# Second level of the down product for chunk 0 of experts 1 to 3, with the down-weight sums right after the up-weight sums

## The chip, the cores and the metric

The kernel runs on one core of a Trainium2 chip. The metric is the device time of one execution in microseconds (us); lower is better. The engines of the core appear in the profile as PE (TensorE matmul), PEld (TensorE weight load), DVE (VectorE), ACT (ScalarE), POOL (GpSimd) and SP (SyncE, which here only issues DMAs).

## The reference

Two blocks follow each other. The first is an attention without softmax with a normalised output; the second weighs four expert networks by probabilities. All arrays are float32.

```python
kv  = einsum('bhsd,bhse->bhde', k, v)              # 8 batches, 8 heads, 576 rows, 64 columns
o   = einsum('bhsd,bhde->bhse', q, kv)
x   = (o / sqrt(mean(o*o, -1) + 1e-6) * g_norm)    # then reshaped to x: 4608 x 512
p   = domain_probs / (domain_probs.sum(-1) + 1e-9) # 4608 x 4
out = sum over e of p[:, e] * (relu(x @ w1[e]) @ w2[e])   # w1: 4 x 512 x 1024, w2: 4 x 1024 x 512
```

Nearly all arithmetic is in the two products per expert, called the up product (x @ w1) and the down product (h @ w2).

## The kernel before

**Tiling and stages.** The 4608 rows of x are cut into NCH = 9 chunks of 512 rows. A stage `s = e*9 + c` is the work of expert `e` (0 to 3) on chunk `c` (0 to 8), so there are 36 stages. Expert 0 also computes the attention that makes the chunks and keeps them, with their sums, in DRAM; experts 1 to 3 load them again (`x_again`).

**Strassen's scheme.** Products are made by the Strassen-Winograd scheme: seven products in place of eight, at the price of sums of the operands before and of the products after. In `up` (from line 851) two levels are used in every stage but the first: 7 outer times 7 inner products, each of two 128x128x128 matmuls (line 881). The down product exists in two forms:

- `down` (from line 1077) uses one level: for each of two halves of rows `t`, seven products (`MERGED` order) of four matmuls with 256 columns each (line 1095). `merge` (lines 1042 and 1049) takes each product from its PSUM bank, scales it by the probability and adds it to the output tile.
- `down_deep` (from line 1117) uses two levels. Seven outer products in four groups, (1, 6), (7, 5), (4, 2) and (3), each with seven inner products of two matmuls with 128 columns per outer product (line 1170). Before them VectorE or GpSimd makes sums of the hidden tiles (`ht`, by `combine`, line 360); between and after them ScalarE copies (line 1198) and VectorE adds (lines 1206 and 1236) put the products together.

**Which stage uses which.** Expert 0 always uses `down`; experts 1 to 3 use `down` for chunks 0 and 8 and `down_deep` for chunks 1 to 7.

**Weights.** While stage `s` with `c = 8` of expert `e` runs, the weights of expert `e + 1` are loaded and summed. `weights_1` loads the four quarters of w1 and makes 4 first-level and 28 second-level sums (buffers `w1y`). `weights_2` loads the four quarters of w2 and makes 4 first-level sums; the function `inner` that it returns makes the 28 second-level sums of w2 (128x256 each, buffers `w2y`), which only `down_deep` reads. The `w2y` buffers are made of room that the attention leaves free: `kv`, `kvbd` and `x_rem`.

**What sets the order.** The program is recorded as operations with a key (a place in units of stages) and an estimate of their cost, and `Plan.layout` turns them into one order per engine. Matmuls go by key, taking the next one that is ready within 0.7 of a stage; VectorE, ScalarE and GpSimd take the ready operation that is due first; SP issues loads by key, and only when a buffer is free. Sums marked `port` (lines 360 and 1236) are kept from running at the same time on VectorE and GpSimd. Buffers (`big`, 29 and later 33 of 128x1024; PSUM kinds `u1`, `u2`, `db`, `ab` of two banks each) are given out in that order too. The down product of stage `s` has keys from `s + 1.2` on: it is interleaved with the up product of stage `s + 1`.

**Bank order.** In `down_deep` ScalarE copies one product into a second PSUM bank and PE accumulates onto the copy (the seed). The seed must land in a bank that PE has already written wide enough; `inner_last` holds a reference to earlier groups for that.

Of the kernel before, what the change touches and what calls it, by code (L numbers as in the profile page):

```python
# [230 lines left out]
def kernel(  # L231
# [36 lines left out]
    nc = tc.nc  # L268
# [3 lines left out]
    P = nc.NUM_PARTITIONS  # L272
# [4 lines left out]
    NCH = B + 1  # L277
    HN = NT // 2
# [13 lines left out]
    ident = const.tile([P, P], F32, name="ident")  # L292
# [41 lines left out]
    plan = Plan()  # L334

    def pe(products, columns, passes=2):
        return {"PE": passes * products * (0.008 + 0.0008125 * columns) + 0.003}
# [4 lines left out]
    def act(n):  # L342
        return {"ACT": 0.155 + 0.00088 * n}

    def either(n):
        return {"DVE": 0.155 + 0.00104 * n, "POOL": 0.15 + 0.00225 * n}
# [9 lines left out]
    def combine(key, cost, out_, a, b, op, reads, writes):  # L356

        plan.add(
            key, cost,
            lambda eng: adder(eng).tensor_tensor(out=out_(), in0=a(), in1=b(), op=op),  # L360
            reads=reads, writes=writes, port=True,
        )

    def load(key, buf, dst, src, kb, reads=(), also=()):
        plan.add(
            key, SPC, lambda eng: nc.sync.dma_start(out=dst(), in_=src), reads=reads,
            parts=[buf] + list(also), kb=kb,
        )
# [37 lines left out]
    def two(ap):  # L406
        return ap.rearrange("p (k t) -> p k t", k=2)
# [5 lines left out]
    def w2_src(e, uh, dh):  # L413
        rows = moe_w2[e][uh * HF:(uh + 1) * HF, dh * HN:(dh + 1) * HN]
        return rows.rearrange("(kt p) d -> p kt d", p=P)
# [50 lines left out]
    def weights_2(e, key, step, deep):  # L466

        f = {n: Buf("big", f"w2_{e}_{n}") for n in (1, 12, 2, 3, 5, 6, 7, 4)}
        for i, (n, uh, dh) in enumerate(((1, 0, 0), (2, 1, 0), (12, 0, 1), (3, 1, 1))):
            load(  # L470
                key + i * step, f[n],
                lambda n=n: f[n].ap[:].rearrange("p (k d) -> p k d", k=4),
                w2_src(e, uh, dh), 512,
            )

        def form(k_, o, a, b, op):
            combine(
                k_, either(1024), lambda: f[o].ap[:], lambda: f[a].ap[:], lambda: f[b].ap[:], op,
                [f[a], f[b]], [f[o]],
            )  # L480

        form(key + 4 * step, 5, 12, 1, ALU.subtract)
        form(key + 5 * step, 6, 3, 5, ALU.subtract)
        form(key + 6 * step, 7, 3, 12, ALU.subtract)
        form(key + 7 * step, 4, 2, 6, ALU.subtract)
        w2f[e] = f

        def inner():
            w2q[e] = {}
            for j, m in enumerate(OUTER):  # L490
                x, y = f[m], Buf("w2y", f"w2y_{e}_{m}")
                parts = {}
                for n, (dq, uq) in ((1, (0, 0)), (2, (0, 1)), (21, (1, 0)), (4, (1, 1))):
                    parts[n] = (x, lambda x=x, dq=dq, uq=uq: x.ap[:].rearrange(
                        "p (k d) -> p k d", k=4)[:, 2 * uq:2 * uq + 2, dq * P:(dq + 1) * P])
                for n, at in ((5, 0), (6, 1), (3, 2), (7, 3)):
                    parts[n] = (y, lambda y=y, at=at: two(y.ap[:, at * HN:(at + 1) * HN]))
                for o, a, b, op in (
                    (5, 21, 4, ALU.add), (7, 1, 21, ALU.subtract), (6, 5, 1, ALU.subtract),
                    (3, 2, 6, ALU.subtract),  # L500
                ):
                    combine(
                        deep + j / 7, either(HN), parts[o][1], parts[a][1], parts[b][1], op,
                        [parts[a][0], parts[b][0]], [y],
                    )
                w2q[e][m] = parts

        return inner
# [330 lines left out]

    hidden = {}  # L840
    summed = {}
    last, inner_last = [], []

    def four(b):

# [271 lines left out]
    def down_deep(s, e, c):  # L1117
# [8 lines left out]
        for i, group in enumerate(((1, 6), (7, 5), (4, 2), (3,))):  # L1126
# [34 lines left out]
            for j, mm in enumerate(ORDER):  # L1161
                key = at + n * j / 49
                ps = bank[{2: 2, 5: 5, 3: 5}.get(mm, 1)]

                def product(eng, group=group, mm=mm, ps=ps, forms=forms):
                    for o, m in enumerate(group):
                        b, at = forms[m][mm]
                        for kt in range(2):
                            col = at * HN + kt * P
                            nc.tensor.matmul(  # L1170
                                ps.ap[:, o * P:(o + 1) * P], lhsT=b.ap[:, col:col + P],
                                rhs=w2q[e][m][mm][1]()[:, kt, :],
                                start=(mm in (1, 5) and o == 0 and kt == 0), stop=(kt == 1),
                                skip_group_check=True,
                            )

                op = plan.add(
                    key, pe(2 * n, P), product,
                    reads=[b for m in group for b in (w2q[e][m][mm][0], forms[m][mm][0])]
                    + ([ps] if mm == 2 else []),  # L1180
                    **{"parts" if mm == 2 else "writes": [ps]},
                    after=inner_last[-2:-1] if mm == 1 else seeds if mm == 5 else (),
                )
                op.marks, op.seed = (ps, n * P), mm == 2
                if mm == 3:
                    inner_last.append(op)

                def cell(tq, dq, pair=pair, n=n):
                    return pair.ap[:].rearrange(
                        "p (o b i t) -> p o b i t", o=2, b=2, i=2)[:, 0:n, tq, dq, :]  # L1190

                def group_of(ap, n=n):
                    return ap[:, 0:n * P].rearrange("p (o t) -> p o t", o=n)

                def copy(where, key=key, ps=ps, n=n, group_of=group_of, **kw):
                    return plan.add(
                        key - 0.4, act(n * P),
                        lambda eng: nc.scalar.activation(  # L1198
                            out=where(), in_=group_of(ps.ap), func=ACT.Copy),
                        reads=[ps], **kw,  # L1200
                    )

                def total(tq, dq, src, add_, key=key, n=n, cell=cell, group_of=group_of, outs=outs):
                    plan.add(
                        key - 0.4, dve(n * P),
                        lambda eng: nc.vector.tensor_tensor(
                            out=cell(tq, dq), in0=group_of(src.ap), in1=group_of(add_.ap),
                            op=ALU.add,
                        ),
                        reads=[src, add_], parts=outs,  # L1210
                    )

                if mm == 1:
                    seeds = [copy(lambda b=bank[2], g=group_of: g(b.ap), parts=[bank[2]])]
                elif mm in (6, 7):
                    snap[mm] = Buf("snap", f"ds{mm}_{s}_{i}")
                    copy(lambda b=snap[mm], g=group_of: g(b.ap), parts=[snap[mm]])
                if mm == 2:
                    copy(lambda cell=cell: cell(0, 0), parts=outs)
                elif mm == 7:  # L1220
                    total(1, 1, bank[5], snap[7])
                elif mm == 4:
                    copy(lambda cell=cell: cell(0, 1), parts=outs)
                elif mm == 3:
                    total(1, 0, ps, snap[6])
# [60 lines left out]
    inner = {}  # L1286
    for e in range(E):
        for c in range(NCH):
            s = e * NCH + c
            if e == 0 and c + 1 < B:  # L1290
                attention(c + 1, s - 0.1, 0.8, s + 0.5)
            if e + 1 < E and c == NCH - 1:
                weights_1(e + 1, s + 0.0, 0.12, s + 0.3)()
                inner[e + 1] = weights_2(e + 1, s + 1.0, 0.12, s + 2.5)
            if s + 1 < E * NCH:
                if e == 0 and c + 1 < NCH:
                    x_views[s + 1] = x_forms(c + 1, s + 0.7)
                else:
                    x_views[s + 1] = x_again((c + 1) % NCH, s + (0.05 if e else 0.6), 0.13)
            if s:  # L1300
                up(s, e, x_views.pop(s))
            if c == 1 and e:
                inner[e]()
            if e and 1 <= c < NCH - 1:
                down_deep(s, e, c)
            else:
                down(s, e, c)
# [54 lines left out]
```

## Time and profile before

| What | Value |
|---|---|
| Median of 9 runs | 1737.31 us (1736.73 to 1737.81) |
| The profiled execution's own time | 1737.34 us |
| Its span, first to last instruction | 1735.6 us |
| Granted TensorE clock, mean | 0.998 |
| PE busy | 1725.9 us (99% of the span) |
| PEld busy | 1649.1 us (95%) |
| DVE busy | 1163.3 us (67%) |
| ACT busy | 922.7 us (53%) |
| POOL busy | 640.2 us (37%) |
| DMA | 220.89 MB, mean 127 GB/s |

The busy time of an engine is the time in which at least one of its instructions runs. Matmuls overlap in the array, so a group's mean length (275 ns for 128 columns) is longer than the distance between two starts; the cost of a matmul on a busy PE is read from the chain of work or from whole stages. A float32 matmul appears as two records. Some matmul records can be missing, so counts of matmuls are taken from the program and not from the trace.

### The profile page before, as it was taken

The page shows a single profiled execution, that of the slowest core. Times are in us where ns is not written, and L with a number is a line of the kernel's source. Part 1 is how long each engine was busy: PE and PEld are TensorE (multiplying, and loading weights), DVE is VectorE, ACT ScalarE, POOL GpSimd, SP SyncE. Part 2 cuts the span into 40 slices and gives each one's busy share as a digit, 9 for nine tenths or more (in the row PEclk, how much of TensorE's full clock was granted, in tenths as well). Part 3 has the DMA queues.
Part 4 walks back from the last instruction along what each step waited for, and adds up shares of the span by engine and source line. Part 5 has one row for each costly group of instructions (what it writes and reads, how often), then busy time and mean ns, then how long its engine had stood idle before and what let it go on. Part 6 is the DMA issues. An engine that isn't in the chain of part 4 may idle for free.

```text
span 1735.6 us, 37757 instructions
## 1 busy us (share of the span) xinstructions
PE 1725.9 (99%) x15074; PEld 1649.1 (95%) x15074; DVE 1163.3 (67%) x1836; ACT 922.7 (53%) x2240; POOL 640.2 (37%) x603
## 2 busy tenths in 40 slices
PE   9999999999999999999999999999999999999998
PEld 7699999999999999999999999999999999999997
DVE  4755655565673567777786567777786567777774
ACT  3354544554444455656555456566655456565652
POOL 2421322133334523333345523333346623333331
PEclk9999999999999999999999999999999999999999
DMA  9756443633333343434455434444456434444442
GB/s 237 220 159 192 156 125 122 192 139 135 135 134 98 107 101 101 117 102 118 126 169 130 104 98 110 110 110 110 119 158 150 110 98 110 111 110 107 113 99 49
DMA packets 148592, 220.89 MB, mean 127 GB/s; under 512 B 49600, under 2 KB 90816, under 8 KB 148416
## 3 DMA queue, kind: packets, MB, share of 16 engines
q1 hardware_dynamic: 133312, 191.21, 34.8%
q0 software_dynamic: 15104, 27.27, 10.9%
q8 instruction: 118, 1.93, 0.5%
q14 instruction: 58, 0.48, 0.1%
HBM read 145.30 MB, written 73.14 MB: 126 GB/s over the span
## 4 chain that ended last, share of the span: by engine, by line
PE 99%; POOL 0%; ACT 0%; DVE 0%; issue 0%; POOLq 0%
PE u L881 44%; PE db L1095 17%; PE db L1170 16%; PE ab L1170 10%; PE ab L1095 4%; PE u L968 2%; PE ab L634 1%; PE ab L678 1%; PE ab L1311 1%; PE ab L620 1%; PE ab L660 1%; PE db L660 0%; POOL rt L551 0%; PE ab L722 0%; PE ab L704 0%; PE ab L738 0%
## 5 line engine op out<-in xcount | busy, mean ns | idle before, releaser
L360 DVE TENSOR_TENSOR big<-big,big 128x1024 f32<-128x1024 f32 (+1 forms) x457 | 481.4, 1068 | 42.0 <-ACT big L864 28.0
L881 PE MATMUL u<-xf,big 128*128 128x128 f32 x3392 | 491.9, 275 | 0.0
L881 PEld LDWEIGHTS u<-xf,big 128*128 128x128 f32 x3392 | 439.0, 192 | 3.7
L881 PE MATMUL u<-xf,w1y 128*128 128x128 f32 x2652 | 387.9, 275 | 0.0
L908 DVE TENSOR_TENSOR big<-u,snap 128x256 f32<-128x256 f32 x460 | 194.1, 422 | 285.4 <-PE u L881 195.0
L881 PEld LDWEIGHTS u<-xf,w1y 128*128 128x128 f32 x2652 | 344.4, 192 | 3.3
L900 ACT ACTIVATE snap<-u 128x256 f32<-128x256 f32 x490 | 188.1, 384 | 257.0 <-PE u L881 222.1
L1095 PE MATMUL db<-big,big 128*128 128x256 f32 x1176 | 278.4, 380 | 2.1 <-DVE big L560 2.1
L900 ACT ACTIVATE big<-u 128x256 f32<-128x256 f32 x460 | 176.5, 384 | 122.6 <-PE u L881 85.1
L1095 PEld LDWEIGHTS db<-big,big 128*128 128x128 f32 x1176 | 212.9, 191 | 26.0 <-DVE big L560 2.3
L360 POOL TENSOR_TENSOR big<-big,big 128x256 f32<-128x256 f32 (+1 forms) x140 | 184.3, 1331 | 128.0 <-DVE big L360 43.5
L864 ACT ACTIVATE big<-big 128x1024 f32<-128x1024 f32 x135 | 141.9, 1051 | 6.5 <-DVE big L360 3.8
L1236 POOL TENSOR_TENSOR big<-big 128x512 f32<-128x512 f32 x21 | 26.6, 1268 | 257.5 <-DVE big L360 188.6
L360 POOL TENSOR_TENSOR big<-big 128x512 f32<-128x512 f32 (+1 forms) x57 | 67.0, 1177 | 134.0 <-DVE big L360 100.2
L1065 POOL DMA_DIRECT2D out_dram<-big x106 | 95.0, 967 | 52.0 <-ACT big L1042 32.9
L1170 PE MATMUL db<-big,big 128*128 128x128 f32 x760 | 108.3, 275 | 0.4 <-ACT snap L1198 0.4
L1198 ACT ACTIVATE snap<-db 128x256 f32<-128x256 f32 (+1 forms) x168 | 60.0, 357 | 86.4 <-PE db L1170 81.6
L900 ACT ACTIVATE u<-u 128x256 f32<-128x256 f32 x245 | 90.8, 371 | 25.4 <-PE u L881 4.5
L1170 PEld LDWEIGHTS db<-big,big 128*128 128x128 f32 x760 | 96.3, 192 | 0.6 <-ACT snap L1198 0.6
L547 POOL TENSOR_SCALAR ss<-ss 128x16 f32<-128x16 f32 (+2 forms) x26 | 6.4, 247 | 241.4 <-DVE ss L540 241.1
L1049 DVE SCALAR_TENSOR_TENSOR big<-db,p_all,big 128x256 f32<-128x256 f32 x74 | 35.7, 483 | 87.3 <-PE db L1095 85.6
L1170 PE MATMUL ab<-kv,big 128*128 128x128 f32 x624 | 89.1, 275 | 0.0
(202 smaller groups left out, 2654.5 us busy)
## 6 DMA issues: line engine op xcount, KB each, us to landing
xf<-x SPq DMA_DIRECT2D x108, 512.0 KB, 3.5
out_dram<-big POOLq DMA_DIRECT2D x90, 256.0 KB, 5.6
xf<-x_h SPq DMA_DIRECT2D x81, 256.0 KB, 3.0
xf<-x SPq DMA_DIRECT2D x81, 256.0 KB, 3.1
x<-xf SPq DMA_DIRECT2D x36, 512.0 KB, 6.7
big<-in_moe_w_dram SPq DMA_DIRECT2D x27, 512.0 KB, 5.2
small<-in_q_dram SPq DMA_DIRECT2D x72, 128.0 KB, 4.6
kv<-in_k_dram SPq DMA_DIRECT2D x30, 288.0 KB, 5.0
```

Of the source, the lines that this page charges most:

```text
L360: lambda eng: adder(eng).tensor_tensor(out=out_(), in0=a(), in1=b(), op=op),
L864: lambda eng: nc.scalar.activation(out=b.ap[:], in_=b.ap[:], func=ACT.Relu),
L881: nc.tensor.matmul(ps.ap[:, u * P:(u + 1) * P], lhsT=w1f[e][m][mm][1]()[:, u * P:(u + 1) * P], rhs=views[m][mm][1](), start=(mm in (1, 5) ...
L900: lambda eng: nc.scalar.activation(out=where(), in_=ps.ap[:, 0:HN], func=ACT.Copy),
L908: lambda eng: nc.vector.tensor_tensor(out=block(whole, a, t), in0=src.ap[:, 0:HN], in1=add_.ap[:], op=ALU.add),
L968: nc.tensor.matmul(bank.ap[:], lhsT=two(w.ap[:])[:, kt, ut * P:(ut + 1) * P], rhs=two(xh[dh].ap[:])[:, kt, :], start=(dh == kt == 0), stop ...
L1049: lambda eng: nc.vector.scalar_tensor_tensor(out=cell(i, half), in0=ap(), scalar=prob(), in1=cell(i, half), op0=ALU.mult, op1=ALU.add,),
L1065: nc.gpsimd.dma_start(out=dst, in_=cell(i)[parts, :], accum_op=ALU.add)
L1095: nc.tensor.matmul(ps.ap[:, 0:HN], lhsT=four(h[m])[:, kt // 2, t, kt % 2, :], rhs=w2f[e][m].ap[:, kt * HN:(kt + 1) * HN], start=(m in (1, ...
L1170: nc.tensor.matmul(ps.ap[:, o * P:(o + 1) * P], lhsT=b.ap[:, col:col + P], rhs=w2q[e][m][mm][1]()[:, kt, :], start=(mm in (1, 5) and o == ...
L1198: lambda eng: nc.scalar.activation(out=where(), in_=group_of(ps.ap), func=ACT.Copy),
L1236: lambda eng: adder(eng).tensor_tensor(out=whole(to), in0=whole(a), in1=whole(b), op=ALU.add),
```

## The change

Chunk 0 of experts 1, 2 and 3 uses `down_deep` as well. For that the 28 second-level sums of w2 are recorded one chunk earlier and with earlier keys, the four loads of w2 move from `s + 1.0 ...` to `s + 0.6 ...` (`s` is the last chunk's stage of the expert before) and are 0.1 instead of 0.12 of a stage apart, and the 28 sums move from `s + 2.5` on to `s + 1.3` on. Since in expert 1 the first `down_deep` no longer follows a `down` that has filled the `ab` banks, a new operation `prime` of four 128x128 matmuls with the identity fills them once.

```diff
-    last, inner_last = [], []
+    last, inner_last, primed = [], [], []
...
-                    after=inner_last[-2:-1] if mm == 1 else seeds if mm == 5 else (),
+                    after=(inner_last[-2:-1] or primed) if mm == 1 else seeds if mm == 5 else (),
...
-                inner[e + 1] = weights_2(e + 1, s + 1.0, 0.12, s + 2.5)
+                inner[e + 1] = weights_2(e + 1, s + 0.6, 0.1, s + 1.3)
...
-            if c == 1 and e:
+            if c == 0 and e:
                 inner[e]()
-            if e and 1 <= c < NCH - 1:
+            if e and c < NCH - 1:
+                if not primed:
+                    banks = [Buf("ab", f"prime{i}") for i in range(2)]
+
+                    def prime(eng, banks=banks):
+                        for b in banks:
+                            nc.tensor.matmul(b.ap[:, 0:P], lhsT=ident[:], rhs=ident[:], start=True,
+                                             stop=False, skip_group_check=True)
+                            nc.tensor.matmul(b.ap[:, P:HN], lhsT=ident[:], rhs=ident[:], start=False,
+                                             stop=True, skip_group_check=True)
+
+                    primed.append(plan.add(s + 1.1, pe(4, P), prime, writes=banks))
+                    primed[0].marks = banks[0], HN
                 down_deep(s, e, c)
             else:
                 down(s, e, c)
```

## The prediction

> **What bounds the kernel now.** I read the chain of work that ended last first. On the page it says by engine, then by line:
>
> ```profile
> PE 99%; POOL 0%; ACT 0%; DVE 0%; issue 0%; POOLq 0%
> ```
>
> TensorE is the chain. Whether it also waits inside that chain is answered by the waits of TensorE (who waited for whom, us in total, times, longest):
>
> ```profile
> PE db L1095 <- DVE big L560: 2.1, 1, 2.1
> PE ab L1311 <- POOL ident masks.py:199: 1.4, 1, 1.4
> PE u L881 <- ACT snap L900: 0.6, 1, 0.6
> PE u L881 <- ACT u L900: 0.5, 1, 0.5
> ```
>
> Asked again by windows, all of this lies in the first 90 us; from 460 us to the end, experts 1 to 3, one wait of 0.4 us is left. There the time is the sum of its matmuls, so the price of a matmul is the distance between starts. The chain between 905 and 997 us (start, us, what) has the prices:
>
> ```profile
> 917.11 1.73 PE db L1095 x8
> ...
> 931.11 1.78 PE u L881 x16
> ```
>
> Eight records of 128x256 take 1.73 us: 0.216 each. Sixteen of 128x128 take 1.78: 0.111 each. A float32 matmul is two records.
>
> Whole stages are the better measure, since they hold every gap. The ScalarE copies of line 900 are 35 per up product, so the 1st, 36th, ... of them mark the stages. Busy time by windows (us, then busy PE, PEld, DVE, ACT, POOL with counts, clock, DMA share, GB/s) of two stages with two-level down products, and of the two stages in which the down products of expert 1's last chunk and expert 2's first chunk run:
>
> ```profile
> 729.60:817.20 87.60, 87.60 (x787) 87.60 (x787) 66.39 (x101) 53.40 (x135) 31.32 (x29) 1.00 0.43 109
> 905.10:997.40 92.30, 92.30 (x635) 86.94 (x634) 54.94 (x76) 45.15 (x106) 52.30 (x59) 1.00 0.49 121
> ```
>
> Both are full of TensorE at the same clock, both hold two up products, and they differ by 4.70 us: **a first-level down product costs 2.35 us more than a second-level one.**
>
> **The sum, part by part.**
>
> *Matmuls replaced.* A first-level product is 14 products of 4 matmuls, 112 records x 0.216 = 24.2 us. A second-level one is 49 x 2 matmuls, 196 records x 0.1117 = 21.9 us (0.1117 is 87.60 / 784, as such a pair of stages holds 4 x 196 records). By records the gain is 2.3, by stages 2.35. Three stages change: 3 x 2.35 = **7.05 us removed**. The order of the built changed kernel has just these counts: 168 matmuls of line 1095 fewer and 294 of line 1170 more.
>
> A rule of the Trainium skill speaks against this edit. "Perfetto Trace Analysis", section Matmuls, holds that larger matmuls are more efficient than smaller ones. The rows agree in sign: 0.1117 / 128 = 0.87 ns per column against 0.216 / 256 = 0.84, some 3%. Were the small ones as cheap per column, the gain would be 3 x 3.0 = 9 us; with the rows it is the 7 us above. The saving of an eighth of the arithmetic outweighs it.
>
> *The new priming matmuls.* Four, so 8 records of 128 columns: 8 x 0.1117 = **0.9 us added**, once. They wait for both `ab` banks; in the order they stand where expert 0's last down product uses `db` alone, so I take no wait. Bounds: 0.4 (if one record each) to 2.5 (if they also wait for one 0.4 us copy at each bank).
>
> *Vector work of the new form.* Per changed stage VectorE or GpSimd get 7 sums of 512 columns (0.68 us, row of line 360) and 14 of 256 (0.41), 7 of line 1236 (0.69) and 8 of line 1206 (six of 0.42, two of 0.28), and lose 6 merges of line 1049 (0.48): 10.5 + 4.8 + 3.1 - 2.9 = 15.5 us of VectorE time. ScalarE gains 20 copies of about 0.36. Nothing of it is on the chain while it keeps ahead. The stage in which it will lie, up of chunk 1 beside down of chunk 0, is the third line here; an ordinary two-level stage is the fourth:
>
> ```profile
> 861.80:905.10 43.30, 43.30 (x390) 43.30 (x390) 37.00 (x55) 25.38 (x66) 21.29 (x22) 1.00 0.58 171
> 905.10:951.30 46.20, 46.20 (x327) 43.73 (x326) 30.88 (x42) 24.02 (x58) 26.58 (x26) 1.00 0.58 138
> 951.30:997.40 46.10, 46.10 (x310) 43.21 (x310) 24.06 (x34) 21.14 (x49) 25.72 (x34) 1.00 0.40 103
> 1040.60:1085.30 44.70, 44.70 (x403) 44.70 (x402) 33.57 (x51) 27.99 (x70) 16.28 (x15) 1.00 0.43 107
> ```
>
> VectorE is busy 24.1 of 46.1 us and most of GpSimd's 25.7 are second-level sums of w2, which move away. What is left is like the fourth line, in which TensorE does not wait. So I put this at nothing.
>
> *The w2 sums, moved one stage forward.* They go into the second line: the first five of the 28 begin there already (GpSimd rows from 933.9 us on), so 23 come in addition, 23 x 0.41 = 9.4 us if VectorE makes them, 23 x 0.73 = 16.8 if GpSimd does. The built order gives VectorE 18 and GpSimd 10 of the 28 for experts 2 and 3. 18 x 0.41 = 7.4 brings VectorE to 38.3 of 46.2 us, a share of 83%; GpSimd stays below its 26.6, as it loses some up-weight sums too. The first line has 37.0 of 43.3, 85%, and no wait of TensorE. The two together matter as well, for they hold each other up: in the first line 128x1024 sums on VectorE last 1.37 us in the mean, and one of them 2.31, against 1.21 for the shortest.
>
> "SBUF — State Buffer", section "two separate sides", calls the port pair that VectorE and GpSimd share an exclusive lock. By that the two busy times of the second line would be added: 30.9 + 26.6 + 9.4 = 66.9 us against 46.2, and TensorE would wait 20 us per expert; but already before they add up to 57.5 without a wait, since sums from PSUM and scaled merges run beside.
>
> In the order all up-weight sums (`w1y`) on VectorE now stand ahead of all down-weight sums for experts 2 and 3, and are done a seventh of a stage earlier than before (14 on VectorE, 7 on GpSimd, against 11 and 10). What waits behind the moved sums is only the next down product, which needs them. Cost nothing, with a bound of 16.8 us per expert.
>
> *Where TensorE could catch up.* One place of the order is new: three to four sevenths into the up product of chunk 0 of experts 2 and 3, TensorE has 20 up matmuls in a row, and then five first-level down products with only two up matmuls between. Before, 6 to 8 up matmuls and one product of four alternate. From the beginning of the stage before up to the end of this place TensorE has 69.8 us of matmuls in both orders (by the two prices), VectorE's queue holds 55.6 us against 51.9 (shortest lengths). In the seventh itself it is 9.6 against TensorE's 11.8. So VectorE still is ahead, by less: I allow **0.2 us** in all for it, between 0 and 5 us per expert, nearest to the second line's zero.
>
> *The w2 loads.* Four issues per expert, 512 KB each; in experts 2 and 3 each stands four issues earlier in SP's queue, ahead of loads of x. The DMA share was 0.58 in the first line; 2 MB more in 43 us is 49 GB/s on 171. SP spends its time waiting for TensorE to free a buffer of x (1022 us in all), so it is ahead of need. Nothing; a load of w2 that waits for its buffer would hold back x by some such wait, 11.1 us at the longest.
>
> Sum, against the profiled execution: 1737.34 - 7.05 + 0.9 + 0.2 = 1731.4. Its own time is within 0.03 of the median.
>
> **The rivals.** About 0.2%, 3.5 us, is what a measurement of this kernel tells from no change: faster is below 1733.8, slower above 1740.8.
>
> *Part is given back (1732.5 to 1737).* VectorE is late at the new place of experts 2 and 3, and TensorE waits 1 to 3 us in each. For it: the 85% line, and the bunched order. Against it: zero waits before.
>
> *The first groups wait for the w2 sums: no gain.* The last of these sums stand in VectorE's queue 0.2 of a stage after the first second-level matmuls are due. If each of the three new products waited as long as it saves, 2.35 us, only the priming would be left: 1738.2. This is also the case in which the change does not do what it says. Against it: the order has up matmuls between them, which TensorE takes while they are ready.
>
> *Slower.* The moved sums and VectorE's own totals (line 908, which frees the up banks) collide at the new place: if GpSimd makes the sums at 0.73 and VectorE is held for most of it, 16.8 us per expert stand ahead of totals, and the five down products cover 5 x 1.73 = 8.6 of it. Two such transitions lose 2 x 8.2 = 16.4: 1731.2 + 16.4 = 1747.6. It decides from 4.8 us per transition on. Against it: the order leaves GpSimd only 10 of the 28.
>
> **How the numbers follow.** The forecast, with under 1.2 us lost, 60%: 1730.3 (priming at 0.4, 2.45 per stage) to 1732.5. Part given back 22%, about two fifths of it still below 1733.8. No gain 10%, slower 8%. Faster is 0.60 + 0.09 + 0.01 for a small piece of the third case = 0.70; same 0.22; slower 0.08. The range must leave out no more than 2 in 10: from 1730.3 through most of the second case to 1736.5.
>
> **What would show it.** Right: TensorE's waits still under 6 us; the two stages around each expert's beginning last 90 us instead of 92.3, the new one 43.8; 33 to 34 us of VectorE in it. Wrong: new lines "PE u L881 <- DVE big" or "PE ab/db L1170 <- DVE kv" with some us, and a VectorE near full in the stage before. A gain well beyond 7 us would mean that the price per stage was misread.

## The result and the profile after

| What | Before | After |
|---|---|---|
| Median of the runs made side by side | 1737.19 us (30 runs) | 1731.42 us (10 runs, 1730.84 to 1731.73) |
| Ratio after to before | | 0.9966, 95% interval 0.9958 to 0.9974 |
| Profiled execution, own time | 1737.34 us | 1730.86 us |
| Its span | 1735.6 us | 1729.1 us |
| DVE busy | 1163.3 us (67%) | 1223.0 us (71%) |
| POOL busy | 640.2 us (37%) | 617.4 us (36%) |

The kernel became 5.77 us faster; 1731.4 had been forecast. On the page of the changed kernel the chain of work that ended last is still TensorE:

```profile
PE 99%; POOL 1%; DVE 0%; ACT 0%; issue 0%; POOLq 0%
```

The waits of TensorE in the changed kernel, from 400 us to the end (who waited for whom, us in total, times, longest), have only the line that the kernel before has too:

```profile
PE db L1170 <- ACT snap L1198: 0.4, 1, 0.4
```

So no wait for the added work shows on the chain. Where the time went is seen in the stages, marked as before by every 35th copy of line 900. Busy time by windows of the changed kernel (columns as in the prediction): the last chunk of expert 1, then the two stages that hold the down products of that chunk and of expert 2's first chunk, one by one and together:

```profile
859.90:903.20 43.30, 43.30 (x390) 43.30 (x389) 37.02 (x57) 23.74 (x64) 21.52 (x20) 1.00 0.66 195
903.20:949.40 46.20, 46.20 (x326) 43.72 (x326) 38.21 (x59) 26.06 (x61) 24.01 (x24) 1.00 0.51 115
949.40:993.50 44.10, 44.10 (x382) 43.69 (x381) 35.78 (x56) 23.39 (x58) 16.08 (x18) 1.00 0.33 97
...
903.20:993.50 90.30, 90.30 (x706) 87.41 (x706) 73.99 (x115) 49.45 (x118) 40.09 (x42) 1.00 0.42 106
```

The pair lasts 90.30 instead of 92.30 us. The stage after it became shorter as well; before and after:

```profile
997.40:1040.60 43.20, 43.20 (x374) 42.79 (x373) 30.08 (x46) 23.09 (x57) 12.74 (x12) 1.00 0.36 99
993.50:1036.40 42.90, 42.90 (x386) 42.90 (x385) 32.80 (x51) 25.43 (x66) 15.01 (x14) 1.00 0.44 111
```

By the unrounded marks that is 1.96 and 0.33 us, **2.29 us per expert**. The same two differences stand in the traces at the beginnings of experts 1 and 3; the first stage of expert 1, which has the priming, is 0.89 us longer, and the other stages from 460 us up to the mark of the last one last alike to 0.01 us. The columns of VectorE and GpSimd show the price that stays hidden: VectorE went from 30.88 to 38.21 us in the second line and from 24.06 to 35.78 in the third, GpSimd from 25.72 to 16.08 in the third.

The new place of the order is where the chain in order of time of the changed kernel (start, us, what) has these pieces:

```profile
915.63 4.47 PE u L881 x40
920.10 1.73 PE db L1095 x8
921.83 0.44 PE u L881 x4
922.27 1.73 PE ab L1095 x8
924.00 5.18 PE db L1095 x24
929.18 0.89 PE u L881 x8
```

They are the 20 up matmuls (40 records), then five one-level products with two up matmuls between. Each piece starts where the one ahead ends: 5.18 us is 24 x 0.216. The bunch cost nothing.

### The profile page after: what moved, and what is told of

Its sections match the earlier page's. It is cut to its first block, busy times and chain, and to the rows that moved or that the text cites. A ratio compares the mean times of both kernels' runs of the same rounds, so it can differ in the third digit from the quotient of the medians.

```text
span 1729.1 us, 38448 instructions
## 1 busy us (share of the span) xinstructions
PE 1719.2 (99%) x15334; PEld 1651.5 (96%) x15334; DVE 1223.0 (71%) x1968; ACT 939.5 (54%) x2300; POOL 617.4 (36%) x561
## 4 chain that ended last, share of the span: by engine, by line
PE 99%; POOL 1%; DVE 0%; ACT 0%; issue 0%; POOLq 0%
PE u L881 45%; PE db L1170 19%; PE db L1095 15%; PE ab L1170 12%; PE ab L1095 2%; PE u L968 2%; PE ab L634 1%; PE ab L1323 1%; PE ab L620 1%; PE ab L678 1%; PE ab L660 1%; POOL rt L551 0%; PE db L660 0%; PE ab L722 0%; PE ab L704 0%; PE ab L738 0%
## 5 line engine op out<-in xcount | busy, mean ns | idle before, releaser
L360 DVE TENSOR_TENSOR big<-big,big 128x1024 f32<-128x1024 f32 (+1 forms) x449 | 440.8, 995 | 35.0 <-ACT big L864 23.8
L881 PE MATMUL u<-xf,big 128*128 128x128 f32 x3104 | 453.0, 275 | 0.0
L881 PEld LDWEIGHTS u<-xf,big 128*128 128x128 f32 x3104 | 401.3, 192 | 2.2
L908 DVE TENSOR_TENSOR big<-u,snap 128x256 f32<-128x256 f32 x430 | 181.3, 422 | 235.6 <-PE u L881 176.2
L1095 PEld LDWEIGHTS db<-big,big 128*128 128x128 f32 x1136 | 205.9, 190 | 25.4 <-DVE big L560 2.3
L1170 PE MATMUL db<-big,big 128*128 128x128 f32 x1056 | 146.8, 275 | 0.4 <-ACT snap L1198 0.4
L1170 PEld LDWEIGHTS db<-big,big 128*128 128x128 f32 x1056 | 132.1, 192 | 0.6 <-ACT snap L1198 0.6
L1198 ACT ACTIVATE snap<-db 128x256 f32<-128x256 f32 x192 | 68.5, 357 | 99.9 <-PE db L1170 95.0
L1170 PE MATMUL db<-kv,big 128*128 128x128 f32 x804 | 114.6, 275 | 0.0
L1170 PEld LDWEIGHTS db<-kv,big 128*128 128x128 f32 x804 | 102.1, 192 | 0.1
L1206 DVE TENSOR_TENSOR big<-ab,snap 128x256 f32<-128x256 f32 x140 | 59.1, 422 | 57.4 <-ACT snap L1198 31.9
```

Source lines behind the costliest of these rows:

```text
L881: nc.tensor.matmul(ps.ap[:, u * P:(u + 1) * P], lhsT=w1f[e][m][mm][1]()[:, u * P:(u + 1) * P], rhs=views[m][mm][1](), start=(mm in (1, 5) ...
L908: lambda eng: nc.vector.tensor_tensor(out=block(whole, a, t), in0=src.ap[:, 0:HN], in1=add_.ap[:], op=ALU.add),
L1095: nc.tensor.matmul(ps.ap[:, 0:HN], lhsT=four(h[m])[:, kt // 2, t, kt % 2, :], rhs=w2f[e][m].ap[:, kt * HN:(kt + 1) * HN], start=(m in (1, ...
L1170: nc.tensor.matmul(ps.ap[:, o * P:(o + 1) * P], lhsT=b.ap[:, col:col + P], rhs=w2q[e][m][mm][1]()[:, kt, :], start=(mm in (1, 5) and o == ...
L1198: lambda eng: nc.scalar.activation(out=where(), in_=group_of(ps.ap), func=ACT.Copy),
L1206: lambda eng: nc.vector.tensor_tensor(out=cell(tq, dq), in0=group_of(src.ap), in1=group_of(add_.ap), op=ALU.add,),
```

## The experiments

All were run in five rounds beside the kernel before. Its median was 1737.07 us in the first four, 1737.33 in the next four and 1737.29 in the last four, so a difference between medians of different rounds is known to some 0.3 us.

To see waits of TensorE more finely than the list of waits does, I add up in each trace, from 470 us on, what the distance between two starts is above 0.1117 us (128 columns) or 0.216 (256 columns), where that is over 0.03 us. I call it *lost starts*. It is 1.07 us before and 1.07 after, all of it in the last stage, where no up product is left.

**1. The moved loads and sums alone.** Two levels only for chunks 1 to 7 again; the priming stays.

```diff
-            if e and c < NCH - 1:
+            if e and 1 <= c < NCH - 1:
```

> The changed kernel with chunk 0 of experts 1 to 3 back on the one-level down product; the earlier loads and sums of w2 and the priming (now before chunk 1 of expert 1) stay. Theory (the time is the sum of TensorE's matmuls, and moving loads and sums costs nothing): the time before plus the priming, 1737.2 + 0.9 = 1738.1. Rival (the earlier sums bring or cost something by themselves, for instance by clearing VectorE in chunk 1): 1735 or below, or 1740 and above.

Measured: 1738.21 us, ratio to before 1.0006 (0.9997 to 1.0015); lost starts 1.07. The move brings and costs nothing that can be measured; what is left is the priming. In the trace only one stage between 460 us and the mark of the last one differs from before, the one with the priming, by 0.89 us. Against this kernel, which differs from the changed one in nothing but the three down products, the changed one is 6.79 us faster: 2.26 us per stage, against the 2.29 of the traces.

**2. Without expert 1.** One level in chunk 0 of expert 1, and no priming.

```diff
-            if e and c < NCH - 1:
-                if not primed:
+            if e and (c or e > 1) and c < NCH - 1:
+                if not primed and e == 1 and c == 0:
```

> The changed kernel with the two-level product in chunk 0 of experts 2 and 3 only; expert 1 keeps one level there, and nothing is primed. Theory (each stage is worth 2.35 us, the priming costs 0.9): 1737.2 - 2 x 2.35 = 1732.5, that is 1.1 to 1.4 above the changed kernel. Rival (the stages give more than 2.35 each, and the priming or expert 1's beginning loses more than 0.9): equal to the changed kernel or below it, 1731.4 or less.

Measured: 1732.75 us, ratio 0.9975 (0.9966 to 0.9984): 4.32 us for two stages, 2.16 each, and lost starts 1.07. Expert 1's part of the change is worth 1.33 us, a stage less the priming.

**3. Priming ten times.**

```diff
-                        for b in banks:
+                        for b in banks * 10:
```

> The changed kernel with its four priming matmuls done ten times over (36 more, written to the same two banks). Theory (a record of 128 columns costs 0.1117 us wherever it stands on TensorE, and a matmul is two records): 72 x 0.1117 = 8.0 us more than the changed kernel, 1739.5. Rival (TensorE has hidden waits near there, which the extra matmuls fill): less than 5 us more. Rival (identity matmuls are cheaper, one record each): 4 us more.

Measured: 1739.41 us, 7.99 more than the changed kernel for nine more primings: 0.89 each, as worked out from two records per matmul. So neither a hidden wait nor a cheaper identity shows.

**4. Two levels with the old keys.**

```diff
-                inner[e + 1] = weights_2(e + 1, s + 0.6, 0.1, s + 1.3)
+                inner[e + 1] = weights_2(e + 1, s + 1.0, 0.12, s + 2.5)
```

> The changed kernel with the loads and sums of w2 back at their old keys (loads from 1.0 on, sums from 2.5 on), while chunk 0 still uses two levels and so needs them in the same stage. Theory (the order takes what is due first within its reach, and TensorE has the next up product to go on with; the move is needed because keys bound how early a sum may be taken): TensorE waits for sums of w2, some us in each expert; 1732 to 1745. Rival (the move of the sums costs or brings nothing, the order would find the place by itself): 1731.4.

Measured: 1736.06 us, ratio 0.9995 (0.9986 to 1.0004). Four fifths of the gain are gone, so the move is needed. Lost starts are 6.00, that is 4.93 more, which accounts for the 4.64 us. TensorE's waits in this kernel, from 400 us on:

```profile
PE db L1170 <- ACT snap L1198: 1.9, 4, 0.5
PE db L1095 <- DVE big L1049: 0.6, 1, 0.6
PE ab L1095 <- DVE big L1049: 0.6, 1, 0.6
```

No line names a sum of w2. The chain in order of time of this kernel shows one of the waits, in the second stage of expert 2:

```profile
985.00 0.91 PE db L1170 x8
985.91 0.02 issue
985.93 0.39 ACT snap L1198
986.32 0.04 issue
986.37 1.16 PE db L1170 x8
```

Two products on the same `db` bank follow each other with no up matmul between, and 0.46 us pass while ScalarE copies the first. The order had put the second-level products late and close together, because their sums came late; the chip then waits for the bank, not for the sum. Of the 4.93 us about 1.5 are in the last stage (the two lines of 1095), the rest around the beginnings of the experts. The same 1.5 us in the last stage come back in experiments 8, 9 and 12. In these four orders the last stage but one lasts 42.9 us and in all others 44.7; why VectorE's merges are late behind it stays open.

**5 and 6. All 28 sums on one engine.** In `inner`, `either(HN)` becomes `gp(HN)` or `dve(HN)`.

> The changed kernel with all 28 second-level sums of w2 per expert bound to GpSimd (now VectorE has 18 of them in experts 2 and 3). Theory (GpSimd has room: 10 x 0.73 become 28 x 0.73 us, 13 us more in a stage with some 18 us idle, and VectorE gets 7 us back): the changed kernel's time, 1731.4, at most 2 us above. Rival (sums on GpSimd hold up VectorE's totals at the start of experts 2 and 3, the slower case of the prediction): TensorE waits up to 8 us per expert there, 1736 to 1748.

> The changed kernel with all 28 second-level sums of w2 per expert bound to VectorE. Theory (10 more sums of 0.41 us in a stage where VectorE has 6 us or more left): the changed kernel's time, 1731.4. Rival (VectorE is at its limit in that stage): TensorE waits 1 to 4 us per expert for VectorE, 1734 to 1743.

Measured: 1731.99 us on GpSimd, ratio 0.9969 (0.9956 to 0.9981), and 1731.67 on VectorE, ratio 0.9967 (0.9955 to 0.9980); lost starts 1.34 in both. Both theories hold. The second window above (its ends are the marks of the changed kernel; those of these two kernels lie up to 1 us off), with the sums on GpSimd and then on VectorE:

```profile
903.20:949.40 46.20, 46.19 (x325) 43.53 (x324) 32.03 (x47) 24.31 (x60) 28.54 (x31) 1.00 0.50 115
```

```profile
903.20:949.40 46.20, 46.20 (x328) 43.77 (x328) 37.45 (x61) 24.87 (x60) 23.87 (x21) 1.00 0.51 115
```

TensorE is busy for the whole window with VectorE at 32 or at 37 us. The prediction's slower case, GpSimd's sums holding up VectorE's totals, does not come even where GpSimd makes them all. VectorE was not brought nearer to its limit by this: in the window it is busy 37.45 us, and 38.21 in the changed kernel, since the order gave other sums to GpSimd, which is as busy without any of the 28 (23.87 and 24.01 us).

**7. The sums twice.** Each second-level sum of w2 is made twice, with the same outcome.

```diff
+                  for again_ in range(2):
                     combine(
                         deep + j / 7, either(HN), parts[o][1], parts[a][1], parts[b][1], op,
```

> The changed kernel with each of the 28 second-level sums of w2 made twice, so 28 x 0.41 = 11.5 us more of VectorE (or 28 x 0.73 = 20.4 of GpSimd) per expert, in the very stretch where they stand. It measures how far the changed kernel is from a wait of TensorE. Theory (there is slack, but less than this): TensorE waits, some us per expert; 1733 to 1750. Rival (slack is ample, the order spreads the sums over the stage): 1731.4.

Measured: 1732.95 us, ratio 0.9974 (0.9964 to 0.9984): 1.53 more than the changed kernel. Lost starts are 2.65, 1.58 more, 0.79 in each of experts 2 and 3. TensorE's waits from 400 us on (lines are one higher in this kernel) show for whom:

```profile
PE u L882 <- ACT snap L901: 0.9, 2, 0.5
PE db L1171 <- ACT snap L1199: 0.4, 1, 0.4
```

Again it is a bank turned round without cover, this time of the up product. So 28 more sums per expert cost TensorE less than 1 us, and the time lies just under the range of the theory, which had some us per expert. VectorE did not become fuller, though: the order gave it 47 of the 56 sums and moved other sums to GpSimd. In the four stages from the last chunk of expert 1 on, VectorE was busy 140.2 us and GpSimd 89.1; in the changed kernel it was 143.8 and 76.6.

**8. Two levels in chunk 8 of experts 1 and 2 too.**

```diff
-            if e and c < NCH - 1:
+            if e and (c < NCH - 1 or e < E - 1):
```

> The changed kernel with two levels also in chunk 8 of experts 1 and 2, the stage beside which the next expert's weights are summed. Theory (TensorE's matmuls alone: 2 x 2.35 us less): 1726.7 if VectorE, GpSimd and the seven buffers of w2's sums keep up. Rival (the sums of the next w2 have to wait for those buffers, which the last chunk's product now still reads, and VectorE gets 15.5 us more in its fullest stage): TensorE waits more than it saves, 1733 to 1750.

Measured: 1735.11 us, ratio 0.9986 (0.9977 to 0.9995), 3.69 slower than the changed kernel. The two stages save 2 x 2.26 = 4.5, and lost starts grow to 9.41, 8.34 more: 8.34 - 4.5 = 3.8. TensorE's waits, from 400 us on:

```profile
PE u L881 <- DVE big L908: 2.6, 3, 1.0
PE ab L1170 <- ACT ab L1198: 0.6, 1, 0.6
PE u L881 <- ACT u L900: 0.6, 2, 0.3
PE ab L1095 <- DVE big L1049: 0.6, 1, 0.6
PE db L1095 <- DVE big L1049: 0.6, 1, 0.6
PE db L1170 <- ACT snap L1198: 0.5, 1, 0.5
```

Here a wait on VectorE's totals is first: 2.6 us, or 3.4 of the 8.34 in lost starts. Waits on ScalarE's copies are another 3.4, and 1.5 are in the last stage. In the second stage of expert 2 VectorE is busy 39.0 of 45.1 us.

**9 and 10. Loads and sums apart.** One argument of the call of `weights_2` at a time goes back: `weights_2(e + 1, s + 0.6, 0.1, s + 2.5)`, then `weights_2(e + 1, s + 1.0, 0.12, s + 1.3)`.

> The changed kernel with only the keys of the 28 second-level sums of w2 back at the old place (from 2.5 on); the loads stay early (from 0.6 on). It splits the 4.6 us by which the kernel with both at the old keys is slower than the changed one. Theory (the key of the sums is what makes the order take the first groups late and bunched): about 1736, as with both at the old keys. Rival (the loads are what is late): 1731.4.

> The changed kernel with only the loads of w2 back at the old keys (from 1.0 on); the sums keep the new ones (from 1.3 on). Theory (the loads have room, the sums' key decides): 1731.4, at most 1 us more. Rival (the loads are what is late): about 1736.

Measured: 1735.80 us with late sums, ratio 0.9991 (0.9982 to 1.0000), lost starts 5.21; 1730.79 us with late loads, ratio 0.9965 (0.9951 to 0.9978), lost starts 1.07. The key of the sums is what counts; the earlier loads bring nothing. With late loads the kernel is not faster than the changed one either: lost starts are the same and the runs overlap (1730.74 to 1731.42 against 1730.84 to 1731.73). With late sums 4.14 us of starts are lost above the changed kernel, 1.5 of them in the last stage. About 1.0 is a wait on the sums themselves, which does appear here:

```profile
PE db L1170 <- POOL kvbd L360: 0.5, 1, 0.5
```

**11. The last stage too.** `if e and (c < NCH - 1 or e == E - 1)`.

> The changed kernel with two levels in the very last down product too (chunk 8 of expert 3), beside which no up product is left. Theory (a stage gains 2.26 us only while TensorE has matmuls of another product to go on with between a group's bank copies): the gain is lost to waits on ScalarE's copies in the tail, 1733 to 1745. Rival (the stage gains by its matmuls alone): 1729.2.

Measured: 1734.47 us, ratio 0.9985 (0.9976 to 0.9993), 3.05 slower than the changed kernel. Lost starts are 4.09, 3.02 more, nearly all in the last stage: a second-level product that is alone on TensorE waits for ScalarE's bank copies, as the theory says, and for VectorE's sums. Two of these waits in the timeline (start, us, engine, line, what, and in brackets the idle time before):

```profile
1699.56 0.68 PE L1170 MATMUL db<-big,big 128*128 128x128 f32 x4 [0.62 <-ACT snap L1198]
...
1701.01 0.71 PE L1170 MATMUL db<-kv,small 128*128 128x128 f32 x4 [0.76 <-DVE big L1206]
```

That is not the whole of it, for the stage also saves 2.3 us. The rest is behind the last matmul, where VectorE has more left to do:

```profile
1725.76 0.29 DVE L1206 TENSOR_TENSOR small<-db,snap 128x128 f32<-128x128 f32 x1
1726.16 0.69 DVE L1236 TENSOR_TENSOR small<-big,small 128x512 f32<-128x512 f32 x1
1726.88 0.88 DVE L1049 SCALAR_TENSOR_TENSOR big<-small,p_all,big 128x256 f32<-128x256 f32 x2
```

In the changed kernel one merge of 0.48 us stands there. From the last matmul's end to the end of the span it is 7.0 us instead of 4.6; 1.5 of the 2.4 us are VectorE's, the others stand behind its last instruction. So 3.0 - 2.3 + 2.4 = 3.1, against the 3.05 measured. The theory named the first loss and not the second.

**12. Chunk 8, with all sums on GpSimd.** Experiments 5 and 8 together.

> Two levels in chunk 8 of experts 1 and 2 too, and all second-level sums of w2 on GpSimd. In the kernel with chunk 8 but free sums VectorE had 39.0 of 45.1 us in the stage after, and TensorE waited 2.6 us for its totals. Theory (VectorE's totals are late because the sums stand ahead of them): with the sums on GpSimd these waits shrink, 1730 to 1733.5. Rival (the seven buffers of w2's sums are what is late, or GpSimd becomes the bound): 1735 or more.

Measured: 1736.60 us, ratio 0.9995 (0.9987 to 1.0004), slower still. The theory fell: the waits on VectorE's totals did shrink, but the lost starts grew to 10.38.

```profile
PE ab L1170 <- ACT ab L1198: 1.3, 2, 0.6
PE u L881 <- ACT snap L900: 1.1, 2, 0.5
PE u L881 <- DVE big L908: 1.1, 2, 0.8
...
```

The waits moved from VectorE's totals to ScalarE's copies. Whether the seven buffers or GpSimd's pace makes the order bunch there stays open. None of the twelve beats the changed kernel by more than the runs scatter.

## Why the prediction was right

*What bounds the kernel.* Right. The differences of experiments 1 to 9 and 12 from the changed kernel are, to 0.4 us, TensorE's matmuls at their prices and the lost starts; experiment 11 needs the tail as well, and experiment 10 differs by 0.6 with nothing in the trace's matmuls to show for it, as much as the clock of the first 90 us makes (see the end).

*Matmuls replaced, 3 x 2.35 = 7.05.* Right in kind, a little large in size: 6.79 by experiment 1, 2.26 per stage, and 2.29 by the traces. The step that was off is the choice of the two windows: the marks do not stand exactly where a stage's matmuls end, and the third stage (43.21 us before, 42.88 after) also changed. Between marks farther off, 729.6 and 1128.1 us of the kernel before, nine stages last 398.5 us and would last 394.0 with second-level products alone (4.5 pairs of 87.55), so the two first-level ones cost 2.3 us more each. The count by records, 24.2 - 21.9 = 2.3, was the better one. As to "Perfetto Trace Analysis" of the Trainium skill, section Matmuls: by its sentence alone smaller matmuls would have been the worse choice; the 3% per column that the rows gave against them is in the 2.26 already.

*Priming, 0.9.* Right: 0.89 by experiment 3, and no wait. Its upper bound of 2.5 does not follow from its own terms: 0.9 + 2 x 0.4 is 1.7.

*Vector work and moved sums, nothing.* Right as to the cost: TensorE did not wait. That VectorE reached 38.21 us in the second window, where 38.3 had been worked out, is luck. Of its 18 moved sums only 12 lie there (5.9 us); other sums take the rest, above all those of 128x1024 (15 instead of 12). Six (2.5 us) fell into the third window, where VectorE is busy 35.78 us and the prediction had named 33 to 34 as a sign of being right; that stage lasts 44.1 us instead of the 43.8 named. Experiments 5 to 7 show how far off a wait was with an order made anew each time: hardly reached with all sums on either engine (0.27 us more of lost starts), just reached with twice the sums. "SBUF — State Buffer" of the Trainium skill, section "two separate sides", speaks of an exclusive lock, and ties it to some instructions of VectorE and not to all; in the second window VectorE and GpSimd are busy 38.21 + 24.01 = 62.2 us of 46.2 without a wait of TensorE, so the busy times of the two cannot simply be added.

*The w2 loads, nothing.* Right, by experiment 10.

*0.2 for the new place.* Not spent; lost starts are the same to 0.01 us. It made up for most of the 0.26 by which the stages were oversized, so that the sum met the median more closely than its terms did: 1737.2 - 6.8 + 0.9 = 1731.3. That the forecast was met to 0.1 us is luck; the runs of one kernel differ by more.

*The rivals.* The second, that the first groups wait for the sums, is what happens with the old key of the sums (experiments 4 and 9). The prediction named it and put the protection in the right place, the up matmuls between; but the wait that it would bring was described as one on the sums, and at the experts' beginnings it is mostly one on a bank copy in experiment 4, and one on the sums for about 1.0 us in experiment 9. The first rival, VectorE late at the new place, did not come. The third, sums on GpSimd that hold up VectorE's totals, did not come either (experiment 5); waits on these totals lead only in experiment 8, where two more stages have the vector work.

## What to carry to other kernels

When one engine is busy without a gap, price its work by the distance between starts, and check the price over whole stages, with marks that let the spill into the next stage be seen. Saved matmuls are saved time only while TensorE has other matmuls to go on with until a bank is copied and VectorE's totals are made: the same edit gave 2.3 us per stage in three places, and made the kernel 3 to 4 us slower in each of two others (experiments 8 and 11). Where a planner writes the order, a late operand can show as a bunched order, and on the chip as a bank wait (experiment 4); so look for runs of one product in the order, not only for waits on the operand.

## What the runs showed of the hardware

*The clock of the first 90 us.* The profiled execution after is 6.48 us shorter than that before, but about 0.5 of that stands ahead of the first changed instruction (a load of w2 at 493 us): the mark of stage 8 is at 460.7 and 460.1 us. The granted clock of the first 90 us was 0.98 before,

```profile
0.00:90.00 90.00, 85.30 (x944) 62.22 (x945) 52.97 (x112) 32.86 (x79) 31.38 (x35) 0.98 0.86 232
```

and 1.00 after:

```profile
0.00:90.00 90.00, 85.08 (x949) 62.51 (x950) 53.47 (x113) 32.81 (x80) 31.91 (x35) 1.00 0.86 233
```

The ten timed runs of the changed kernel part the same way: two with a mean clock of 1.000 took 1730.84 and 1730.87 us, eight with 0.999 took 1731.02 to 1731.73. So a difference of 0.6 us between two single runs of this kernel says nothing.

*Waits of TensorE are longer than their lines.* In experiment 4 the lines of waits from 400 us on add up to 3.1 us, while the lost starts are 6.00. A matmul of 128 columns is drawn 0.275 us long at a distance of 0.112, so the first 0.16 us of a pause are covered by the drawn length, and the start after a pause came some 0.10 late as well. The wait drawn as 0.47 us at 986.37 us of experiment 4 cost 0.64 + 0.10 in starts.
